# Six banks instead of eight for the first joint layer of an attention and MLP kernel, halves of a two-bank tile kept apart in the second, and a new order table

## The chip, the cores and the metric

The kernel runs on one core of a Trainium2 chip. What is measured is the device time of one execution in microseconds (us). The kernel before took 593.06 us (median of three runs, 593.02 to 594.8).

## The reference

Attention over 4 batches of 12 heads with 448 positions and head width 64, with a tanh cap on the scores, then two dense layers over the 1792 tokens (768 to 2048 to 768) with a smooth gate between them. All inputs and outputs are float32.

```python
scores = scale * np.matmul(q, k.transpose(0, 1, 3, 2))
scores = cap * np.tanh(scores / cap)
scores = scores - np.max(scores, axis=-1, keepdims=True)
attn = np.exp(scores)
attn = attn / (np.sum(attn, axis=-1, keepdims=True) + 1e-09)
attn_out = np.matmul(attn, v)
...
x = attn_out.transpose(0, 2, 1, 3).reshape(B * S, H * D)
h = x @ w_in
g = np.where(h >= 1, h, np.where(h <= -1, 0.0, (h + 1) ** 2 / 4))
out = g @ w_out
```

## The kernel before

Every product of the dense layers is made of three matmuls with fp16 operands, since each operand is held as a high and a low half (high times high, low times high, high times low; `product`, L761 to 773). Work goes by pairs of heads, 24 in all: scores on PE, tanh and exponential on ACT, sums on DVE, the product with v on PE, then `norm` and `divide` (copies on ACT, L486, a chain on DVE, L498, and a spread on PE, L509).

Batches 0 and 1 go through the two dense layers plainly (L579 to 617). Batches 2 and 3 are done together with fewer products: sums and differences of their tiles and of blocks of the weights are made first (on DVE; split into halves on ACT and DVE, L522, L525, L795, L796), and each product then serves two blocks. In the **first joint layer** (L836 to 868) turn i of eight takes three accumulators y, x and z from `new_bank`. Product after product is added into y; between them ACT copies y out (`copy_out`, L778), and PE adds the next product to y only when that copy has read it. `plus` (DVE, L783) adds an accumulator to such a copy. `gate` (ACT L589 and L590, DVE L591) makes the input of the second layer. In the **second joint layer** (L893 to 946) three accumulators `ys`, three `xbs`, three `wbs` and three `zbs` take their names from a list `banks`; `scaled` (ACT, L894) copies out, `plus` adds and DMAs store the results. The last product is cut, for its last two chunks, into columns 0 to 255 and 256 to 447 of the same bank, each part with its own `plus` and its own DMA.

PE's accumulators lie in eight banks of PSUM. Four are tiles of their own (f0, f1, av0, t0); the other four are halves of two tiles, s0 and s1 (here s0a, s0b, s1a, s1b). In the program's names (as f0_140, s0_138) the halves of s0 read alike. Before the change `new_bank` goes round all eight, in the order f0, f1, s0a, s0b, s1a, s1b, av0, t0, three a turn: turn 6 has y in s0a, x in s0b, z in s1a, turn 7 has y in s1b, x in av0, z in t0. The second layer goes on in the same round: ys are f0, f1, s0a; xbs s0b, s1a, s1b; wbs av0, t0, s0b; zbs s1a, s1b, av0.

The order of the instructions on each engine is not made by loops. Each step is put into a plan with a cost; the order in which steps are issued, and the engine of those that may run on ACT or DVE, stands in a packed table, ORDER, that was written out beforehand. `Plan.order` unpacks it. The costs in the code went into making that table; when the program is built they do nothing.

At the end `verdict` (L315 to 329) makes one number, fi, from range checks. Each engine loads it (L1409) and branches over a general version of the program (L1410), which doesn't run here.

Of the kernel before, what the change touches and what calls it, by code (L numbers as in the profile page):

```python
# [21 lines left out]
P = 128  # L22
# [68 lines left out]
    "#m8_DpTQL<j<?|t%!MWJSNH`Vzzg^dpTJA_6JNpaSPUQHAMh*w3H#tRM8v095#PXmcn_8EK0d<A_!geSWBdT`pgums5!ePJ(Hne#PvI~48ya9ke2#CiDptct_!{5iJB*C~;1i63QSm!e!M4~AKVVu+"
    "ho3Pr0lvU#h)CE7qhVu=kL^+6D@=gtaS3+7FZeG;$Eef<|Hfq08($*hNBj#DVj}E=eX$>Az)$!cJ7PxcgfS>Fj>MAKAEQxj%!8#cI%UF9m;?vlXq=9jaRwg1u{Z|vVm>U5NpU8Y!LJyTfZ|YooE;Vj"
    "(KuX+WpNoU$2qtOXJG*>h}E$Mmcz}s5^Lf)Y>Kt8HpZpFv;wzadEAP1FdnVKX4o8C;5Y1yEpa<`!5vr^2jVvDLxZptCZ~hg6}#bJRMZ`Z;CP&XhcE#}p@fu@4r32wYK^hzD8{Cra42dzf<NOiOhl<@"
    "BBr4X)D!3892$o6P-qgK#|s#rCSzLaOBXRU4aa_T3A4}?oQnNvJ}y8*DQF=Mpdn;wHLk&(xCjT5qs2Is*5WQ)hwJe;W~9ZGiPF(9+JL)p5beRecml)GM!bx}sW_FOeYhX9(g+$!N$CofqVP1A5>sZH"
    "M@eWtoy4n{gVIw3%0;zl2}PvRw2=1D0y<2m@H8%^Y*dyiQb`&`qiGrCrZF^@uHhoOjyWk0jid2Yi6+nrT1k0nB2A*nG==if89a-tXf>^&TR4@b(O$ZNRcSfh#Qe06_EP~`OWA2U-J&B@j*e0pT1S=X"
    "7_Fxbw2@BGZ*+j_&`Byth3OzwqfNA#X3!RzNp)!}m8WfVoMzF#RF4i(1*%WCsUcOTrgVx<(-}HTHK-8PqC3=ps?c5fof^?STBn-PY-&#TsWCmEBGiJm(=W7xcG9o3UbUoi^b`F|=jj4nq)T*}uF!XC"
    "MUUtseWK6wkZMv}dQ4wvvuZ+LsWt7QEoz6_r$C{4LQm-#eIrs=DUM>*p0tXqo>M#(U%j9sssp{GS9Fc8(;w7^ZcswikvdUl`jcMM8|p$k)mswvlQPPxpVd3suin!J<y1IzNrhJt)CbzCl+sv~cBw>a"
    "lRB>wtBvX}il{ED3#uy}P)XEoilh>#q$-(8p(3j&DyrJ1wyTROrMjZ7tG_9limuM6Z>k#=qwds$VyMrm9LH2u_@FwfQmJ;-la8t6Dz!?ZcB@{LR;5$NReF^{-B34akBX%-s=ey2`mTD@Np(}*Q@^N8"
    ">X16DGOK^+syd;5Raw-1^+4rO#HZAAl~p}dk5pn_%-Pf-eOf(M*OcO0%JNyod`=Zsw^eNQn|h)0s#hwX%C7!U`PCf-oP;$yj>NyK$o!{D&N29jdaa(S94e>ErE)9eXDS6(=Qk=G3&-Rr{9c9U0?Keo"
    "E}~wlX#7F_rJ{3Gj>WOLs4A@rs<d286;~0sj4Gi@s&xET6;cs7GnZB6RC)EUs=;yjovNwg@kjMZ#o;WRfRl1oPR12fMU|6lb1p8WQgM2&rBd_X>K|2G)#3PDN2TFPs;;Wbl~oVU##K~9uE~u!H#b);"  # L100
    "R6_ou5^+zir!sIJ&dY_krOM73xjENYnYgN|rdp{MT!f2q1Jzn}RXMmAx8#PZIG5n+sx8;!l3YWzQTceSD#&eBY0l4$R4wkyjkz5c;4<7;eO2956IGwPauaT+`f+>JfXj1t)s*}5ARfVmxvA>It9cDK"
    ";~uJ+>Zv-Yj%qCrRu#FI>ZB@gD{jqgxIOn#ow&2=%zafCHGs$QKpx3mxEJ^4!Q4*`QN2}J?ym-@?mU!7sY*Or9o9qD5q(+@<8?etjpFe<gopD$HC%Pz(L902sN;H~8pDTpB3I>(JeDW(BsGOcsExdy"
# [71 lines left out]
def fast_body(ctx, tc, flag, qkp, vp, cap, w_in, w_out, out):  # L174
# [61 lines left out]
    def act(n, fn, r, w):  # L236
        either(r, w, act_(n, fn))
# [1176 lines left out]
```

## Time and profile before

| | |
|---|---|
| Median of three runs | 593.06 us (593.02 to 594.8) |
| Profiled execution | 595.54 us, of which 593.4 us is the span of its instructions |
| PE busy | 573.6 us (97%) |
| DVE busy | 517.6 us (87%) |
| ACT busy | 419.7 us (71%) |
| Mean granted clock of TensorE | 0.995 |

PE is busy for nearly the whole span, so the views that matter are those that say where it isn't: its waits, and the stretches by window. Busy time of a matmul group includes its pipelined end, so that the next row on PE may start before the row above has run out. Times in the rows below are counted from the start of the span; the profiled execution's own time is 2.14 us longer than its span.

### The profile page before, as it was taken

Reading aid. Unit: us, or ns where it says so; the run is one execution under the profiler, and the core shown is the slowest. Engines: PE = TensorE matmul, PEld = TensorE weight load, DVE = VectorE, ACT = ScalarE, POOL = GpSimd, SP = SyncE. Lnnn points to the kernel's source line nnn. Section 1 sums busy time; section 2 is a strip of 40 time slices with the busy share of each in tenths; the row PEclk is TensorE's granted clock in tenths of the full one; section 3 lists DMA queues with packets and bytes.
Section 4 is the critical chain, followed back from the end, with each engine's and each line's share of the span. In section 5 each row is a group of like instructions: output and inputs, shape, how many; then the busy total and the mean of one; then the engine's idle time right before and its main releaser. Section 6 shows DMA issues by size and latency. Waiting matters only on the chain. (4 is left out here: it accounts for less than half of the span.)

```text
span 593.4 us, 10251 instructions
## 1 busy us (share of the span) xinstructions
PE 573.6 (97%) x3824; PEld 281.0 (47%) x3824; DVE 517.6 (87%) x1014; ACT 419.7 (71%) x705; POOL 1.3 (0%) x6
## 2 busy tenths in 40 slices
PE   7989999999999999999999999999999899999995
PEld 3334445454445544554444454445555444455543
DVE  7999999999999999999997865799999978999602
ACT  7999988787565689888989979366978766442000
POOL 0000000000000000000000000000000000000000
PEclk9999999999999999999999999999999999999998
DMA  8868748667877311133699999954755545743302
GB/s 303 321 227 291 273 160 298 214 235 266 276 255 255 112 65 60 65 99 105 201 326 289 334 329 304 291 195 139 225 202 199 176 143 160 236 136 121 114 0 85
DMA packets 56990, 119.92 MB, mean 202 GB/s; under 512 B 4962, under 2 KB 35426, under 8 KB 55394
## 3 DMA queue, kind: packets, MB, share of 16 engines
q1 hardware_dynamic: 56928, 119.16, 59.9%
q8 instruction: 32, 0.52, 0.4%
q14 instruction: 28, 0.23, 0.1%
q10 hardware_dynamic: 2, 0.00, 0.0%
HBM read 91.42 MB, written 27.72 MB: 201 GB/s over the span
## 5 line engine op out<-in xcount | busy, mean ns | idle before, releaser
L773 PEld LDWEIGHTS <-w 128*128 128x128 f16 x726 | 71.2, 98 | 74.3 <-issue 9.0
L395 ACT ACTIVATE e<-s,tsc 128x896 f32<-128x896 f32 (+1 forms) x96 | 85.4, 910 | 12.5 <-PE s L387 7.6
L396 ACT ACTIVATE e<-e,capb 128x896 f32<-128x896 f32 (+1 forms) x96 | 88.8, 948 | 0.5
L579 PE MATMUL f<-x,w 128*128 128x448 f16 x192 | 67.8, 353 | 0.1
L615 PE MATMUL f<-g,w 128*128 128x448 f16 x192 | 67.8, 353 | 0.0
L581 PE MATMUL f<-x,w 128*128 128x448 f16 x192 | 67.7, 352 | 0.0
L617 PE MATMUL f<-g,w 128*128 128x448 f16 x192 | 67.7, 352 | 0.0
L616 PE MATMUL f<-g,w 128*128 128x448 f16 x192 | 67.7, 352 | 0.0
L580 PE MATMUL f<-x,w 128*128 128x448 f16 x192 | 67.7, 352 | 0.0
L387 PE MATMUL s<-spl 64*128 64x448 f16 x432 | 49.6, 352 | 1.5 <-ACT e L395 1.5
L463 PE MATMUL av<-e,vt 128*64 128x448 f32 x216 | 45.8, 550 | 0.8 <-ACT xf L486 0.8
L590 ACT ACTIVATE r<-r 128x448 f32<-128x448 f32 x64 | 36.1, 573 | 1.1
L387 PEld LDWEIGHTS <-spl 64*128 64x128 f16 x432 | 17.4, 94 | 29.6 <-issue 17.6
L276 ACT ACTIVATE w<-z 128x768 f16<-128x768 f32 (+1 forms) x22 | 20.7, 943 | 13.6 <-DVE z L273 13.6
L589 ACT ACTIVATE r<-f,half 128x448 f32<-128x448 f32 x34 | 21.4, 630 | 12.2 <-PE f L581 11.0
L277 DVE SCALAR_TENSOR_TENSOR w<-z,w 128x768 f16<-128x768 f32 (+1 forms) x28 | 29.7, 1062 | 0.3
L579 PEld LDWEIGHTS <-w 128*128 128x128 f16 x192 | 18.8, 98 | 19.4 <-issue 3.9
L615 PEld LDWEIGHTS <-w 128*128 128x128 f16 x192 | 18.8, 98 | 18.7 <-issue 3.0
L617 PEld LDWEIGHTS <-w 128*128 128x128 f16 x192 | 18.8, 98 | 17.5
L581 PEld LDWEIGHTS <-w 128*128 128x128 f16 x192 | 18.8, 98 | 17.6
L424 DVE TENSOR_TENSOR sums<-e,e 128x896 f32<-128x896 f32 x24 | 26.0, 1084 | 0.7 <-ACT e L396 0.7
L346 DVE SCALAR_TENSOR_TENSOR spl<-qkr,spl 128x896 f16<-128x896 f32 (+2 forms) x25 | 26.1, 1047 | 0.3
(318 smaller groups left out, 1141.5 us busy)
## 6 DMA issues: line engine op xcount, KB each, us to landing
w<-w_in SPq DMA_DIRECT2D x32, 384.0 KB, 5.6
z<-w_out SPq DMA_DIRECT2D x24, 512.0 KB, 5.6
w<-w_in SPq DMA_DIRECT2D x14, 768.0 KB, 7.0
qkr<-qkp SPq DMA_DIRECT2D x23, 448.0 KB, 4.7
vt<-vp SPq DMA_DIRECT2D x24, 320.0 KB, 4.5
w<-w_out SPq DMA_DIRECT2D x7, 1024.0 KB, 5.9
zd<-z SPq DMA_DIRECT2D x16, 384.0 KB, 2.6
zd<-z SPq DMA_DIRECT2D x12, 512.0 KB, 4.1
```

What stands on the lines that cost most here:

```text
L387: T.matmul(s[:, j, :S], lhsT=t[h, a, S + c * P:S + (c + 1) * P], rhs=t[h, b, :S], start=(i == 0), stop=(i == 2))
L395: act(w * S + 60, lambda: A.activation(e[:, :w] if c < 3 else e[:, 0].rearrange("p (h s) -> p h s", h=2), s[:, :w, :S] if c < 3 else s[:, ...
L396: act(w * S + 125, lambda: A.activation(e[:, :w], e[:, :w], AF.Exp, scale=capb), ek + [("tsc", None)], ek)
L463: T.matmul(a[h, :S], lhsT=vt[:, j * 3 + c], rhs=e[:, j], start=(c == 0), stop=(c == 2), skip_group_check=True)
L579: T.matmul(ph, lhsT=w1[:, 0, fc, c], rhs=x[c][0][:, 0], start=(c == 0), stop=False)
L580: T.matmul(ph, lhsT=w1[:, 1, fc, c], rhs=x[c][0][:, 0], start=False, stop=False)
L581: T.matmul(ph, lhsT=w1[:, 0, fc, c], rhs=x[c][0][:, 1], start=False, stop=(c == NCC - 1))
L590: act(S, lambda: A.activation(r, r, AF.Square, scale=math.sqrt(WS * XS / GS)), rk, rk)
L615: T.matmul(po, lhsT=hi[:, fc], rhs=gv[:, 0], start=(fc == 0), stop=False)
L616: T.matmul(po, lhsT=lo[:, fc], rhs=gv[:, 0], start=False, stop=False)
L617: T.matmul(po, lhsT=hi[:, fc], rhs=gv[:, 1], start=False, stop=(fc == NFC - 1))
L773: T.matmul(t, lhsT=lhs(x, c), rhs=rhs[c][0][:, y], start=(first and c == i == 0), stop=(stop and c == n - 1 and i == 2), skip_group_check= ...
```

## The change

The table ORDER is a new one. The first joint layer takes its accumulators from six banks of six different tiles (f0, f1, s0a, av0, t0, s1a): even turns have f0, f1, s0a for y, x, z, odd turns av0, t0, s1a. In the second layer ys are f0, f1, av0; xbs s0a, s0b, s1a; wbs t0, s1b, s0a; zbs s0b, s1a, t0. The last product stops in its bank, t0, before the last two chunks and has a `plus` of all 448 columns; the last two chunks go into f0 (columns 0 to 255) and f1 (256 to 447) and are added from there. A dozen costs of the plan are other numbers; two of them are shown. Lines stand one lower after L703.

```diff
...
-    "c-l=^1E3_yvW<w0jLaO{wr$(CZQHhO+qUi9v9TC)ceoh;TU9;#e&0rQB5=-$$hsX11Q23FH~@$P3Jk=Bcn}{fB!CEz5VpBQkQkCcQV0*pAUQ;a6p#`KO29u55mJGJ)Q|?!LON&&f{`FSl!S_q0ir`j"
...
+    "c-mEW1ArvS^L0dIWMt;rwr$(CZQHhO+cs{^yEP7Ln|EvTzV51?`~AP3>8Ywj;KhrVH2|?7HVDK4191UCK|BZt@gV{b2qu7p5D^kVVn_lEksv8pNCr_LIi!G;5FR3fgH#X=QbQU@3nic=q=T|h3MxW+"
...
-        act(width + 110, lambda: A.activation(hi.bitcast(F32), hi.bitcast(F32), AF.Relu, accum_out=chp[:, i, part:part + 1]), zk, zk + [("chp", (i, part))])
+        act(width + 155, lambda: A.activation(hi.bitcast(F32), hi.bitcast(F32), AF.Relu, accum_out=chp[:, i, part:part + 1]), zk, zk + [("chp", (i, part))])
...
-        pe(20 + 800 * len(cs), run, [k for c in cs for k in st["e", n, c][1]] + vk + (ak if cs[0] else []), ak, "aa")
+        pe(-10 + 772 * len(cs), run, [k for c in cs for k in st["e", n, c][1]] + vk + (ak if cs[0] else []), ak, "aa")
...
     retire([("s1", None)], pbk[4:6])
     turn["pb"] = -1
+    pb1, pb1k = [[l[i] for i in (0, 1, 2, 6, 7, 4)] for l in (pbs, pbk)]
 
     def take_from(name, tiles, keys):
         turn[name] = i = (turn.get(name, -1) + 1) % len(tiles)
         return tiles[i], [(keys[i], None)]
 
     def new_bank():
-        t, k = take_from("pb", pbs, pbk)
+        t, k = take_from("pb", pb1, pb1k)
         return t[:, :S], k
...
-        act(S, (lambda: A.copy(u, t)) if scale == 1.0 else lambda: A.activation(u, t, AF.Copy, scale=scale), k, ukey)
+        act(S - 67, (lambda: A.copy(u, t)) if scale == 1.0 else lambda: A.activation(u, t, AF.Copy, scale=scale), k, ukey)
...
-    banks = [new_bank() for _ in range(8)]
+    banks = [(pbs[i][:, :S], [(pbk[i], None)]) for i in (0, 1, 6, 2, 3, 4, 7, 5)]
     ys, xbs, wbs, zbs = banks[:3], banks[3:6], [banks[6], banks[7], banks[3]], [banks[4], banks[5], banks[6]]
...
     def steps(bank, first, lhs, rhs, r):
-        for c0 in range(0, HF, STEP):
-            product(bank, first and c0 == 0, c0 + STEP == HF, lambda x, c, c0=c0: lhs(x, c0 + c), rhs[c0:c0 + STEP], r)
+        for c0 in range(0, len(rhs), STEP):
+            product(bank, first and c0 == 0, c0 + STEP == len(rhs), lambda x, c, c0=c0: lhs(x, c0 + c), rhs[c0:c0 + STEP], r)
...
         steps(zbs[i], True, wv(i, 0), gb(2), wqk(i, 0))
         plus(zbs[i], u4s[i], out_scale)
         store(3, HE + i, u4s[i])
-        if i < HE - 1:
-            steps(zbs[i], False, wv(HE + i, 1), gb(3), wqk(HE + i, 1))
-            plus(zbs[i], u2s[i], out_scale)
+        last = i == HE - 1
+        steps(zbs[i], False, wv(HE + i, 1), gb(3)[:HF - STEP * last], wqk(HE + i, 1))
+        plus(zbs[i], u2s[i], out_scale)
+        if not last:
             store(2, HE + i, u2s[i])
-    (t, k), (u, ukey), lhs, rhs = zbs[i], u2s[i], wv(HE + i, 1), gb(3)
-    for c0 in range(0, HF - STEP, STEP):
-        product(zbs[i], False, False, lambda x, c, c0=c0: lhs(x, c0 + c), rhs[c0:c0 + STEP], wqk(HE + i, 1))
-    for q, cols in enumerate(LAST):
-        bank_, part = (t[:, cols], [(k[0][0], q)]), (u[:, cols], [(ukey[0][0], q)])
-        product(bank_, False, True, lambda x, c: lhs(x, HF - STEP + c), [(g[:, :, cols], key) for g, key in rhs[HF - STEP:]], wqk(HE + i, 1))
-        plus(bank_, part, out_scale)
-        dma(4 * P * (cols.stop - cols.start), lambda cols=cols: M.dma_start(out[DM - P:, 2 * S + cols.start:2 * S + cols.stop], u[:, cols]), part[1], [("out", (2, HE + i, q))])
+            continue
+        u, ukey = u2s[i]
+        for q, cols in enumerate(LAST):
+            bank_, part = (ys[q][0][:, cols], ys[q][1]), (u[:, cols], [(ukey[0][0], q)])
+            product(bank_, True, True, lambda x, c, f=wv(HE + i, 1): f(x, HF - STEP + c), [(g[:, :, cols], key) for g, key in gb(3)[HF - STEP:]], wqk(HE + i, 1))
+            plus(bank_, part, out_scale)
+            dma(4 * P * (cols.stop - cols.start), lambda cols=cols, u=u: M.dma_start(out[DM - P:, 2 * S + cols.start:2 * S + cols.stop], u[:, cols]), part[1], [("out", (2, HE + i, q))])
     retire([(k, None) for k in xlk[6:]], ["z1"])
     verdict()
     with tc.manual_schedule():
```

On PE at the end of the first joint layer, before. The first column is the line; s0, s1, f0, f1, av0 and t0 are accumulators, w2_0 and w2_1 weights of the second layer, qkr, spl and w1 weights of the first, and what follows the arrow is the pair of operands (one row of several chunks shown, each of three matmuls).

```order
L773 MATMUL s0_138<-e1_96,qkr0_89 128x448
...
L773 MATMUL s1_139<-g15_127,qkr1_90 128x448
...
L773 MATMUL s0_138<-x3_108,qkr1_90 128x448
...
L773 MATMUL s0_138<-g1_113,w2_0_80 128x448
...
L773 MATMUL f1_141<-g16_128,w2_1_81 128x448
...
L773 MATMUL s0_138<-x0_105,qkr0_89 128x448
...
L773 MATMUL s1_139<-e0_95,w1_79 128x448
```

The same place after the change:

```order
L774 MATMUL f0_140<-x3_108,qkr1_90 128x448
...
L774 MATMUL f1_141<-g16_128,w2_1_81 128x448
...
L774 MATMUL f1_141<-g8_120,w2_1_81 128x448
...
L774 MATMUL av0_142<-x5_110,w1_79 128x448
...
L774 MATMUL f0_140<-x0_105,qkr0_89 128x448
...
L774 MATMUL s0_138<-e0_95,w1_79 128x448
...
L774 MATMUL s0_138<-g7_119,w2_1_81 128x448
```

Turn 6's y lay in s0a, and the next product on PE went into s0b; now it lies in f0, and twelve matmuls into f1 and nine into av0 stand between y's third product (the row with x3) and its fourth (the row with x0).

On PE in the second layer, before. ys[2] is the s0 of the rows with w2_5 and of those with w1_79 as their second operand; wbs[2] is the s0 of the rows with w2_2.

```order
L773 MATMUL s0_138<-sums0_103,w1_79 128x448
...
L773 MATMUL s0_138<-g0_112,w2_2_82 128x448
...
L773 MATMUL s0_138<-w1_79,w2_5_85 128x448
...
L773 MATMUL s0_138<-sums0_103,w2_5_85 128x448
...
L773 MATMUL s0_138<-w1_79,w2_2_82 128x448
...
L773 MATMUL s1_139<-x3_108,w2_4_84 128x448
```

The same place after the change:

```order
L774 MATMUL av0_142<-sums0_103,w1_79 128x448
...
L774 MATMUL s1_139<-raw_86,w2_4_84 128x448
...
L774 MATMUL t0_143<-x5_110,w2_2_82 128x448
...
L774 MATMUL av0_142<-w1_79,w2_5_85 128x448
...
L774 MATMUL s0_138<-g0_112,w2_2_82 128x448
...
L774 MATMUL t0_143<-e2_97,w2_2_82 128x448
```

ys[2] moved from s0a to av0, and products into other tiles stand between its parts.

On DVE at the end of the program, before:

```order
L326 SCALAR_TENSOR_TENSOR rr0_129<-z1_88,rr0_129 1x4
L328 TENSOR_REDUCE rr0_129<-rr0_129 1x1
L783 SCALAR_TENSOR_TENSOR wr1_137<-av0_142,wr1_137 128x256
L329 TENSOR_SCALAR fi_59<-rr0_129,f_58 1x1
L783 SCALAR_TENSOR_TENSOR wr1_137<-av0_142,wr1_137 128x192
L1409 TENSOR_LOAD fi_59
```

The same place after the change:

```order
L784 SCALAR_TENSOR_TENSOR wr1_137<-t0_143,wr1_137 128x448
L326 SCALAR_TENSOR_TENSOR rr0_129<-z1_88,rr0_129 1x2
L784 SCALAR_TENSOR_TENSOR wr1_137<-f0_140,wr1_137 128x256
L784 SCALAR_TENSOR_TENSOR wr1_137<-f1_141,wr1_137 128x192
L328 TENSOR_REDUCE rr0_129<-rr0_129 1x1
L329 TENSOR_SCALAR fi_59<-rr0_129,f_58 1x1
L1410 TENSOR_LOAD fi_59
```

The number fi, which stood ahead of the last `plus`, now stands behind it. On SP the load of fi stood between the last two DMAs, and now stands behind both.

## Rows read from the trace of the kernel before

**Rows 1.** Windows: stretch, its length, busy time per engine, clock, DMA share, GB/s

```profile
core 0: us, PE busy (x) PEld busy (x) DVE busy (x) ACT busy (x) POOL busy (x), PEclk, DMA share, GB/s
0.00:60.00 60.00, 53.46 (x509) 22.52 (x510) 54.69 (x143) 53.94 (x69) 0.66 (x5) 1.00 0.81 286
60.00:285.00 225.00, 225.00 (x1621) 110.63 (x1621) 221.19 (x337) 175.63 (x257) 0.00 (x0) 1.00 0.52 179
405.00:465.00 60.00, 60.00 (x319) 31.02 (x317) 57.74 (x118) 48.99 (x96) 0.00 (x0) 1.00 0.62 203
474.77:478.43 3.66, 3.66 (x12) 1.56 (x12) 3.53 (x9) 3.44 (x6) 0.00 (x0) 0.61 0.42 139
495.00:516.00 21.00, 19.26 (x100) 9.54 (x99) 18.45 (x41) 9.21 (x18) 0.00 (x0) 1.00 0.62 189
```

**Rows 2.** Waits of PE: line <- what ended it: total us, times, longest

```profile
PE s L773 <- ACT xf L778: 2.7, 1, 2.7
PE t L509 <- DVE mix L498: 2.2, 2, 1.9
...
PE s L773 <- ACT w L522: 1.2, 1, 1.2
...
PE s L773 <- ACT wr L894: 0.6, 1, 0.6
PE s L773 <- ACT xf L894: 0.6, 1, 0.6
...
PE s L773 <- ACT wr L778: 0.5, 1, 0.5
PE av L773 <- DVE w L796: 0.4, 1, 0.4
```

**Rows 3.** Timeline of PE at turn 6: start, duration, what [idle before]

```profile
470.77 1.30 PE L773 MATMUL s<-e,qkr 128*128 128x448 f16 x6
474.77 2.40 PE L773 MATMUL s<-g,w 128*128 128x448 f16 x6 [2.70 <-ACT xf L778]
476.96 1.64 PE L773 MATMUL f<-g,w 128*128 128x448 f16 x6
```

**Rows 4.** Timeline of ACT at the same place

```profile
474.20 0.51 ACT L778 COPY xf<-s 128x448 f32<-128x448 f32 x1
```

**Rows 5.** Timeline of PE and of DVE at turn 7's gate

```profile
489.27 1.86 PE L773 MATMUL s<-x,spl 128*128 128x448 f16 x9
...
497.42 0.62 DVE L591 SCALAR_TENSOR_TENSOR vt<-s,r 128x448 f32<-128x448 f32 x1 [2.23 <-PE s L773]
497.96 0.61 DVE L783 SCALAR_TENSOR_TENSOR wr<-t,wr 128x448 f32<-128x448 f32 x1
...
500.11 0.62 DVE L591 SCALAR_TENSOR_TENSOR wr<-wr,r 128x448 f32<-128x448 f32 x1
```

**Rows 6.** Timeline of PE, behind that gate

```profile
501.39 1.01 PE L773 MATMUL s<-w,w 128*128 128x448 f16 x3 [1.18 <-ACT w L522]
```

**Rows 7.** Timeline of all engines at the end

```profile
585.61 0.49 PE L773 MATMUL av<-sums,w 128*128 128x256 f16 x3
586.13 0.42 DVE L783 SCALAR_TENSOR_TENSOR wr<-av,wr 128x256 f32<-128x256 f32 x1 [2.73 <-PE av L773]
586.48 0.19 DVE L329 TENSOR_SCALAR fi<-rr,f 1x1 int32<-1x1 f32 x1
586.61 0.41 PE L773 MATMUL av<-e,w 128*128 128x192 f16 x3 [0.52 <-DVE wr L783]
...
587.30 0.36 DVE L783 SCALAR_TENSOR_TENSOR wr<-av,wr 128x192 f32<-128x192 f32 x1 [0.64 <-PE av L773]
```

**Rows 8.** The branch, by line: engine, operation, ns min/median/max, first and last start

```profile
L1410 PEldq COMPARE_BRANCH  x1: 3977/3977/3977, 587.3 to 587.3; - x1
...
L1410 DVEq EVENT_SEMAPHORE  x1: 21/21/21, 591.5 to 591.5; - x1
```

**Rows 9.** Timeline of PE in the head

```profile
31.52 0.35 PE L509 MATMUL t<-mix,sel 128*128 128x224 bf16 x2 [1.90 <-DVE mix L498]
31.80 0.97 PE L463 MATMUL av<-e,vt 128*64 128x448 f32 x4
```

More of the change, by code (lines that the diff above doesn't have):

```diff
@@ L91 @@
[L91 to L102, printed above, removed]
@@ new lines @@
+    "hz=Pb24sYokO>+>IVcU8p%PSsEYJwDg28N19%?~t_yjE=DpZE*PzJI?W3Z?p2ULKnPzN05ges5=YCsbRhb^HdgvX{(7urH@Xax~488(1skOziBeP{=H;WG?_e9#d(L3?Np_23J%f&B0lIzs`N1K*(_"
+    "w1zP-7KTG1_y#d>E{uSYP#BV9Hz)!>pa&F%agYT&z*LwBqhK0zf$>lbQs6w81jV5zbcgAX5*NdKSOC2sCiaHOFd8Pnen^cgpbt!eB@hey!b<1|OW^>_fHg1>20?%53Ikvv%!WfS3l_n0h>fdYEnI+K"
+    "VKp3vbx;Tg!!o!CX)rDhfsODRoP{HB5;j9BTn`5!9v*{p5C>;M1-t~OU<+)5({LV+!*#d}N1+X#fHSZawn0|h4m%(lZh)QeJ7mY*a0B+h73hUG;TPBi*YG+%fWmkc?!aC66MjNHyaf;89z24Zm;;Mo"
+    "QTz*@!Zmn-f53Kk3#Z|2xDPM!IqZcyco+YMocI|2ffrB=U%~^-g}3n)yoM+E5G&$7h=@<|9aO^CSR8NQGq{g$;61#BNB9ArVP$-SRj?|4gnRf3-(d-?j}0&qzQ<}98UKYS7!@1hCrpcgS1}qsM#M;z"
@@ new lines @@
+    "4hb7$bZm?5a0EVq`1lsn<7ZTu0iR=gOo0Dj6a0o5u_GqL{a6wcA!8|QgdZ?6eZdY`8aH8LEQ6h}H-5!FI1>9}Zp?$DFd0RqzcC3e!S9$C|HaYx5i{XwOo~4+ALhsYn4F@}Sd2z7XdEKNq|8_ViN;_-"
+    "9Ds4CI+n#6*c6*#Ka5L2(P=ssCq+y%P?OM7Oh75ACf35(G!tV{ZH!0dusj+{MYC`jmZ0X?0%zlLOhYX(9Ie2g*crRv9PC4NFd@~&%{UOZ;7SZngRm<mq6`$DTH#hqOWklVc1KIAFbVa*A$R~&Q%2f`"
+    "t#Ld~z=JpxGtnVDf{wOhPn?TMX)sO1c{mJHP&(Rylkg}W#xpn>v(Q-_j_0s1&BxWa02ksKJdY)53f88n*pGh4MYtAs;yU~T*JFRmOuyi-xC`gdZ@2-o(qbGyyKym<q9L>qkKs@nM#Jei?!kdHi1uP>"
+    "noD&kJ!PY^bOLkG2&zbb;z-(u^XMd&qcW73>e3P#MN26H&8JFKmCDm!SeY(hHCjdyDHr9Wi#VFb&{!Hr<7om-q)9ZHrqEQHM!RVNRiPDh3UkwRT22co57nbZl$R<{ecD6$s5&*IrnHg{(Is3(`Drz+"
@@ L131 @@
+    "x#Hi140$I5Ls;vE$zWhu*q2Z8RmJZI4`|OZ`^$V{V~EmTG5v~otU;f)!6?|*1kbmBL{eBN-uW9yS<vfW2?ps4HvC_mW`B2pMqU!&pJ-v^!vA%#cdoDxf~SU|^EB*q2|G{7mne@O-mS+_A3lcvbLs|#"
+    "E|{-h3D1|W1i@m5_~uJa(1rLC9CqUPO7E+>A3ys?MxZ}L{95^^aacrNH~3oTYXf_Y=@AM-C%D&s6oL~xrKbPXHF$V%=#7Sa`g?f$$fF;>-_G7b@Ido=-FpjwuyQhnBsbU)zEXI`{MV(xRfP@*Uv(+O"
+    "N$`$@kl|neKw;eWHH-eIHQ;ad&r1k<_wZHFCk8_(6aIfmkM<J"
 )
@@ L388, in qk @@
         parts = range(len(cuts(n)) if cs[-1] > 1 else 1)
-        pe(sum(570 if c < 3 else 385 for c in cs), run, [(k, (z, i)) for z in parts for i in range(2)], [x for c in cs for x in st["s", n, c][1]], "qr" if cs[-1] == 3 else "qq")
+        pe(sum(572 if c < 3 else 322 + 95 * (len(cs) > 1) for c in cs), run, [(k, (z, i)) for z in parts for i in range(2)], [x for c in cs for x in st["s", n, c][1]], "qr" if cs[-1] == 3 else "qq")
     def expo(n, c):
@@ L450, in run @@
                             T.matmul(a[h, :S], lhsT=vh[:, x, j * 3 + c], rhs=e[:, y, j], start=(c == x == y == 0), stop=(c == 2 and x == 1), skip_group_check=True)
-            pe(20 + 570 * len(cs), run, [k for c in cs for k in st["eh", n, c][1]] + vk + (ak if cs[0] else []), ak, "aa")
+            pe(32 + 570 * len(cs), run, [k for c in cs for k in st["eh", n, c][1]] + vk + (ak if cs[0] else []), ak, "aa")
             return
@@ L484, in run @@
                     T.matmul(t[q:q + 32, :S // 2], lhsT=w, rhs=m, start=(g == 0 and c is None), stop=(g == 1 and c == (late[-1] if late else None)), tile_position=(0, q))
-        pe(450 + 375 * len(late), run, mk + [k for c in late for k in st["e", n, c][1]] + [("ones", None), ("halves", None)] + (tk if g else []), tk, "tt")
-        act(S, lambda: A.copy(xf, a[:, :S]), ak, fk)
+        pe(402 + 385 * len(late), run, mk + [k for c in late for k in st["e", n, c][1]] + [("ones", None), ("halves", None)] + (tk if g else []), tk, "tt")
+        act(S - 67, lambda: A.copy(xf, a[:, :S]), ak, fk)
         if g:
```

75 lines of the change are left out of this document (38 added, 37 removed).

## The prediction

> **What bounds the kernel now.** I read the windows first [rows 1]. PE, DVE and ACT stand beside each other there: from 60 to 285 us PE is busy for all of 225.00, and from 405 to 465 for all of 60.00 with 319 matmuls, 0.188 us each at a granted clock of 1.00. PE is the bound, its matmuls are the same ones after the change, and a change of order can only give back time in which PE is idle or slow. So the next view is the list of PE's waits [rows 2], and then the timeline around each of the longer ones. The reader is to ask of each wait whether what it waits for is needed by the matmul that waits.
>
> Most of them are not. At 474.77 PE has waited 2.70 us for ACT's copy of turn 6's y [rows 3, 4], but the matmul goes into another bank, s0b, where nothing has to be copied; y lies in s0a, the other half of the same tile. The wait is for the tile. The twelve matmuls behind it run from 474.77 to 478.43 at a mean granted clock of 0.61, so for the most part at the lower level of 1.2 GHz [rows 1], after that idle time. The waits for L894 (twice 0.6) and for the copy wr L778 (0.5) have the same form: the waiting product goes into one half of s0, the copy reads the other [rows 2].
>
> The wait before 501.39 is the end of a longer chain. DVE's gate reading of turn 7's y, in s1b, has waited 2.23 us for a product into s1a [rows 5]. Behind it on DVE stands an addition of 0.61, behind that, by way of ACT, the next gate at 500.11, and behind that ACT's cast L522 that PE waits 1.18 us for [rows 6].
>
> **The change part by part.**
>
> *Clock and waits at turn 6.* y now lies in f0 and the product that follows in f1, tiles of their own. Between y's third and fourth product stand 12 and 9 matmuls, 21 x 0.188 = 3.95 us. PE's last matmul of the third product ended at 472.07 and the copy at 474.71, 2.64 us later [rows 3, 4]; 3.95 covers that, with 1.3 over. The wait of 2.7 goes. Twelve matmuls at 0.188 take 2.26 us and took 3.66; without an idle time before them I take the other clock, 1.4. The 1.4 rests on the clock falling after long waits only: waits of 1.90 and 1.18 [rows 9, 6] lie in stretches whose mean granted clock is 1.00 [rows 1]. If this cover fails, 2.7 and 1.4 stay. Sum: 4.1, bounds 0 and 4.1.
>
> *Waits for the other half of a tile.* With s0a and s1a alone in the first layer, the 0.5 goes; with ys[2] in av0, the 1.2 of L894 goes. ys[2] itself is read by ACT between two of its products; twelve matmuls (2.26 us) into s1 and t0 stand there now, where PE waited 0.6 with none, so nothing is late next. Sum: 1.7, bounds 0.5 and 1.7.
>
> *Turn 7's gate.* It no longer waits 2.23 for a neighbour, so the wait of 1.18 at the end of the chain goes. Next in line is the weight split L796 on DVE, for which PE waited 0.4 a little later [rows 2]; I leave that wait in. Sum: 1.2, bounds 0 and 1.6.
>
> *Six banks instead of eight.* A bank comes back after two turns, not after eight thirds of one. Counted in the new order, the matmuls between a bank's last product of one turn and its first two turns on are 36 to 60 (6.8 to 11.3 us), but once, for av0 from turn 5 to turn 7, only 21, 3.95 us. There PE waits for a gate on DVE. Before, turn 7's last product ended at 491.13 and its gate at 498.04, 6.9 later, of which 2.23 was the wait for the neighbour [rows 5]: 4.7 without it. PE then waits 4.7 - 3.95 = 0.8. Behind the waiting matmul stand all products of turn 7 on PE. In a shorter form the same can happen where only six to nine matmuls stand between a product and the next into the same accumulator; for these I take another 0.4, the size of the wait for L796. Cost 1.2, bounds 0 and 13.4 (the last rival below).
>
> The Trainium skill, in Perfetto Trace Analysis, section Matmul Optimizations, asks for all 8 PSUM banks to be used so that as much as possible runs side by side; the change leaves two idle in the first joint layer. By the rule eight in rotation would be the better choice, and the trace agrees only in part: the copies of [rows 3, 4] kept a seventh and an eighth bank from being used while they ran. By the rule alone nothing of the 8.0 below would arrive; I don't follow it here, and it is a rival.
>
> *The last product.* Its second half of columns waited 0.5 for DVE to read the first half of the same bank [rows 7]; in f0 and f1 that wait goes. A `plus` of 448 columns is added, 0.61 as at 497.96 [rows 5], in a stretch where DVE had idled 2.73 [rows 7]. But fi is now made after the last `plus`, before it was done at 586.67. PE's branch takes 3.98 us from 587.30 and ends at 591.28, and DVE goes on at 591.5 [rows 8]. The end of PE's 256 columns lies at 586.10. In the new order the 192 columns follow at once (586.76, as 0.66 passed from 586.61 to 587.27), the `plus` lasts 0.36 to 587.15, and a reduction (0.1, an estimate: half of L329's time) and L329 (0.19) bring fi to 587.4, 0.7 later than before. The branch of PE would end at 592.0, 0.5 behind DVE's 591.5. I take a loss of 0.4, between that and 0 (if the branch is not what ends last); bounds a gain of 0.5 (PE's wait, if the last DMA ends it all) and a loss of 0.7 (all of fi's delay).
>
> *The head.* PE waited 1.90 at 31.52 for DVE's chain of `divide` [rows 9]. In the new order a product of the same kind as that of 31.80 (0.97) stands ahead of the first L509. It fills 1.0 of the wait. ACT is busy for 53.94 of the first 60 us and DVE for 54.69 [rows 1], so more than that can hardly come; bounds 0 and 1.9.
>
> *Costs in the code, fewer or more casts on DVE against ACT.* The costs do nothing on the chip. A cast moved between the two is hidden behind PE, as PE is idle nowhere from 60 to 285 us; if that cover were gone it would cost about 0.6, as DVE's work of 448 columns does [rows 5].
>
> *Sum.* 4.1 + 1.7 + 1.2 + 1.0 = 8.0 given back, 1.2 + 0.4 lost, 6.4 net. From the profiled execution, 595.54 with a span of 593.4 and 2.14 around it, that is 589.1. The median of the runs lies 2.48 below the profiled execution, at 593.06; from there it is 586.7.
>
> **The rivals.**
>
> *DVE takes over the bound (589.8).* From 405 to 465 us DVE is busy for 57.74 of 60, from 495 to 516 for 18.45 of 21 [rows 1]. When PE no longer stands still at turn 6, DVE has to keep up through turns 6 and 7 with no time to recover. All that it surely gains itself is the 2.23 of the false wait. Then of the 5.3 of turn 6 and 7's gate (4.1 + 1.2) only 2.2 arrives: 6.4 - 3.1 = 3.3. For it: these shares, and the wait for L796 that stays. Against it: DVE had waited for PE (2.23) and not only PE for DVE.
>
> *Other things are late at the same places (593.0).* The matmul at 474.77 may also wait for operands that come just as late, as ACT was busy with other work until 474.20; the wait then carries another name. What remains is the 0.5 and the 1.2, less 1.6: no change. Against it: ACT's work ahead of the copy is not what PE's next matmul reads by its row.
>
> *Six banks are too few (slower, 598.9).* If gates lag by 9.5 us behind their last product (the measured 6.9 and the 2.6 of a copy queued in front), PE waits 9.5 less the cover wherever this is short: 5.5 at the cover of 3.95, 2.7 at 6.8, 1.0 twice at 8.5, 0.4 at 9.1: 10.6, and twice 1.4 of clock behind the two long ones, 13.4 in all. In place of the 1.2 that is 593.06 - 8.0 + 0.4 + 13.4 = 598.9. It decides from a lag of about 8.4. Against it: 2.23 of the 6.9 is the wait that goes, so that the lag should be nearer to 4.7. The rule of the Trainium skill on the banks, named above, points to this side.
>
> **How the numbers follow.** Forecast 0.66; DVE bound 0.20; no change 0.08; slower 0.06. Two runs of this kernel within 0.3% (1.8 us) can't be told apart. The first two cases are faster by more than that, at 586.7 and 589.8; so 0.86, 0.08, 0.06. The range reaches down to 583.0, where nothing of the 1.6 is lost and the head gives all its 1.9 and more is found in the order, and up to 591.5, past DVE as the bound; the last two cases lie outside.
>
> **What would show it.** Right: no wait of PE over 1 us from 390 to 585; a clock of 1.00 from 465 to 480; no waits of PE for L894's line; the matmul into f1 directly behind that into f0 at the end; the gate's reading of turn 7 within 5 us of its last product. Wrong: PE waits for DVE's gate line in front of products into av0 or f0 (six banks too few); DVE without idle time from 465 to 516 and PE waiting for L796 or its casts (DVE bound); a new wait where 2.70 stood.

## The result and the profile after

The kernel after took 585.86 us (median of four runs, 584.97 to 586.69) against 593.93 (593.02 to 597.16) for the kernel before in the same comparison; the ratio is 0.9854, with a 95% interval of [0.9812, 0.9896]. Measured again in the last series of experiments it was 585.04 against 594.67, ratio 0.9842 [0.9826, 0.9859]. So the change gives 8.1 to 9.6 us by the medians, and 9.4 with a margin of 1 by the narrower interval. 586.7 was forecast, a change of 6.4 from 593.06. The time that an execution takes beyond its span is 2.1 to 2.3 us in all 56 runs of the kernel before that stood beside the experiments, and 2.2 to 3.3 in the nine of the kernel after; so the span fell a little more than the time, from 592.5 to 582.3 in the last series.

First the list of PE's waits, the whole of it (the columns are those of [rows 2]):

```profile
PE s L387 <- ACT e L395: 1.6, 3, 1.0
PE f L639 <- POOL x L633: 1.2, 1, 1.2
PE t L509 <- DVE mix L498: 0.7, 1, 0.7
PE av L463 <- ACT e L396: 0.2, 1, 0.2
PE t L484 <- DVE sums L424: 0.2, 1, 0.2
PE s L384 <- ACT e L395: 0.2, 1, 0.2
```

All of these lie in the first 60 us. No line of the joint layers is left: the 2.7, the 1.2, the 0.5 and both 0.6 of [rows 2] are gone, and so is the 0.4 for L796 that I had left in. Against [rows 1] the windows show the same:

```profile
0.00:60.00 60.00, 55.50 (x514) 22.95 (x515) 54.74 (x142) 54.32 (x70) 0.66 (x5) 1.00 0.81 292
...
390.00:465.00 75.00, 75.00 (x398) 38.83 (x397) 72.00 (x150) 57.77 (x112) 0.00 (x0) 1.00 0.60 192
465.00:516.00 51.00, 51.00 (x272) 26.35 (x270) 50.26 (x108) 34.35 (x66) 0.00 (x0) 1.00 0.60 192
516.00:574.00 58.00, 58.00 (x308) 30.01 (x307) 33.56 (x83) 8.03 (x15) 0.69 (x1) 1.00 0.29 98
```

PE is busy for all of 390 to 574 us, at a granted clock of 1.00 throughout. DVE is busy for 50.26 of the 51 us from 465 to 516: it comes close to PE, and doesn't hold it up.

Turn 6 and turn 7 on PE, then the gates of turn 5 and of turn 7 on DVE:

```profile
466.79 1.30 PE L774 MATMUL f<-e,qkr 128*128 128x448 f16 x6
467.92 2.43 PE L774 MATMUL f<-g,w 128*128 128x448 f16 x12
470.19 0.73 PE L774 MATMUL av<-x,w 128*128 128x448 f16 x3
...
483.81 1.87 PE L774 MATMUL av<-x,spl 128*128 128x448 f16 x9
```

```profile
468.17 0.61 DVE L591 SCALAR_TENSOR_TENSOR wr<-av,r 128x448 f32<-128x448 f32 x1
...
488.03 0.61 DVE L591 SCALAR_TENSOR_TENSOR vt<-av,r 128x448 f32<-128x448 f32 x1
```

Twelve matmuls stand behind y's third product, as in [rows 3]; there they took 3.66 us at a clock of 0.61 [rows 1], here they pass from 467.92 to 470.19, in 2.27. Turn 5's gate has read av0 by 468.78, 1.4 before PE comes back to that bank at 470.19. Turn 7's gate ends at 488.64, 3.0 behind the end of its last product (485.68), where it was 6.9 in [rows 5].

The end of the program:

```profile
574.61 0.49 PE L774 MATMUL f<-e,w 128*128 128x256 f16 x3
...
575.27 0.41 PE L774 MATMUL f<-e,w 128*128 128x192 f16 x3
...
575.54 0.78 DVE L784 SCALAR_TENSOR_TENSOR wr<-f,wr 128x256 f32<-128x256 f32 x2
575.99 0.81 SPq L947 DMA_DIRECT2D out<-wr  x2
...
576.45 0.20 DVE L329 TENSOR_SCALAR fi<-rr,f 1x1 int32<-1x1 f32 x1
```

The wait of [rows 7] in front of the 192 columns is gone, and the last addition ends at 576.3. But from the first product of 256 columns (574.61) to the end of the span (583.4) 8.8 us pass; in the kernel before these were 8.1 (from 585.28 to 593.4). This part became longer, though SP, the engine that ends last, branches at almost the same distance from that product as before: 3.1 us behind it, 3.0 in the kernel before. What grew is the time from SP's branch to its next step, 3.8 against 3.1 (rows in the experiments with the early verdict). From that step to the end 1.9 us pass in every trace of this case.

### The profile page after: what moved, and what is told of

It reads as the page before. It is cut to its first block, busy times and chain, and to the rows that moved or that the text cites. A ratio compares the mean times of both kernels' runs of the same rounds, so it can differ in the third digit from the quotient of the medians.

```text
span 583.4 us, 10253 instructions
## 1 busy us (share of the span) xinstructions
PE 571.3 (98%) x3824; PEld 281.0 (48%) x3824; DVE 518.6 (89%) x1017; ACT 420.9 (72%) x703; POOL 1.3 (0%) x6
## 4 chain that ended last, share of the span: by engine, by line
PE 53%; DVE 4%; ACT 1%; issue 0%; ACTq 0%
PE s L774 12%; PE f L774 11%; PE av L774 7%; PE t L774 3%; PE f L615 3%; PE f L616 3%; PE f L617 3%; PE av L463 2%; PE s L387 2%; PE f L579 1%; PE f L580 1%; PE f L581 1%; PE av L369 1%; PE t L484 1%; DVE wr L591 1%; DVE g L525 0%
## 5 line engine op out<-in xcount | busy, mean ns | idle before, releaser
L774 PEld LDWEIGHTS <-w 128*128 128x128 f16 x726 | 71.0, 98 | 65.4
L589 ACT ACTIVATE r<-f,half 128x448 f32<-128x448 f32 x36 | 22.6, 627 | 9.1 <-PE f L581 8.5
L579 PEld LDWEIGHTS <-w 128*128 128x128 f16 x192 | 18.8, 98 | 19.4 <-issue 3.6
L615 PEld LDWEIGHTS <-w 128*128 128x128 f16 x192 | 18.8, 98 | 18.2 <-issue 2.3
L617 PEld LDWEIGHTS <-w 128*128 128x128 f16 x192 | 18.8, 98 | 17.5
L581 PEld LDWEIGHTS <-w 128*128 128x128 f16 x192 | 18.8, 98 | 17.5
L580 PEld LDWEIGHTS <-w 128*128 128x128 f16 x192 | 18.8, 98 | 16.1 <-issue 0.4
```

Of the source, the lines that this page charges most:

```text
L579: T.matmul(ph, lhsT=w1[:, 0, fc, c], rhs=x[c][0][:, 0], start=(c == 0), stop=False)
L580: T.matmul(ph, lhsT=w1[:, 1, fc, c], rhs=x[c][0][:, 0], start=False, stop=False)
L581: T.matmul(ph, lhsT=w1[:, 0, fc, c], rhs=x[c][0][:, 1], start=False, stop=(c == NCC - 1))
L615: T.matmul(po, lhsT=hi[:, fc], rhs=gv[:, 0], start=(fc == 0), stop=False)
L617: T.matmul(po, lhsT=hi[:, fc], rhs=gv[:, 1], start=False, stop=(fc == NFC - 1))
L774: T.matmul(t, lhsT=lhs(x, c), rhs=rhs[c][0][:, y], start=(first and c == i == 0), stop=(stop and c == n - 1 and i == 2), skip_group_check= ...
```

## The experiments

The theory at the start was that of the prediction: PE waited for the other half of a tile. Rivals: DVE sets the pace of the joint layers anyway; or only the new order matters.

**Two banks exchanged in the kernel before.** The order is untouched.

```diff
+    pbs, pbk = [[l[i] for i in (0, 1, 2, 6, 4, 5, 3, 7)] for l in (pbs, pbk)]
     turn["pb"] = -1
```

> The kernel before, its order untouched, with two of its eight accumulator banks exchanged (s0b and av0), so that turn 6's y (s0a) and the product behind it no longer lie in one tile; turn 7's y and the product behind it (s1b, s1a) still do. Theory one, that PE waited for the tile and not for the bank: the waits of 2.7, 0.5 and twice 0.6 go and the clock stays at its upper level, 5.8 us faster (4.5 to 6.5), with the wait of 1.2 near 501 still there. Rival one, that DVE bounds these turns: 2 to 3.5 faster, and PE waits for DVE's weight splits or gates. Rival two, that only the new order table frees these places: within 1 of before, with a wait of about 2.7 at the same place.

Measured: 592.03, ratio 0.9952 [0.9934, 0.9970], 2.9 us faster. PE's timeline at turn 6, then its longest waits in the joint layers:

```profile
471.75 1.30 PE L774 MATMUL s<-e,qkr 128*128 128x448 f16 x6
472.88 1.30 PE L774 MATMUL av<-g,w 128*128 128x448 f16 x6
...
475.75 0.92 PE L774 MATMUL s<-x,qkr 128*128 128x448 f16 x4 [0.43 <-ACT xf L779]
```

```profile
PE s L774 <- ACT r L590: 1.6, 1, 1.6
...
PE s L774 <- DVE qkr L797: 0.6, 1, 0.6
```

With another tile the product follows y's at once (472.88), so the 2.7 was for the tile. But half of the gain doesn't arrive: PE waits 0.43 for the same copy where it really needs it, 0.6 for a weight split on DVE, and 1.6 more. The view puts the 1.6 down to ACT, whose work ended last, at 481.99. In the program the waiting product doesn't depend on that work; it depends on DVE's addition, which ended at 481.98:

```profile
481.36 0.62 DVE L784 SCALAR_TENSOR_TENSOR vt<-s,vt 128x448 f32<-128x448 f32 x1
```

```profile
482.04 0.73 PE L774 MATMUL s<-x,spl 128*128 128x448 f16 x3 [1.59 <-ACT r L590]
```

The addition reads turn 6's z, in s1a, and the product is one of turn 7's y, in s1b: the halves of s1 still meet. A wait of 0.62 at 421.35 is of the same form, with a product into s0a and a copy that reads s0b. So 2.2 of the 2.9 us that are missing are again waits for the other half of a tile, and the longer of them is as long as it is because DVE makes two weight splits ahead of its addition. The first theory is right about the wait; what it had wrong is that this exchange leaves no other such wait behind.

**All halves four places apart, in the kernel before.**

```diff
+    pbs, pbk = [[l[i] for i in (0, 1, 2, 4, 6, 7, 3, 5)] for l in (pbs, pbk)]
     turn["pb"] = -1
```

> The kernel before, its order untouched, with the eight banks permuted so that the halves of a tile are four places apart in the rotation; turn 7's gate no longer shares a tile with the product behind it either. Theory one: as in the run with two banks exchanged, and the 1.2 near 501 goes too: 7.0 us faster (5.5 to 7.5). DVE as the bound: 2 to 3.5 faster. The order table alone: within 1 of before.

Measured: 595.73, ratio 1.0007 [0.9994, 1.0020]. Theory one expected 7.0 faster and fails. The old waits are replaced by others:

```profile
465.73 0.62 DVE L784 SCALAR_TENSOR_TENSOR vt<-s,vt 128x448 f32<-128x448 f32 x1
```

```profile
466.40 2.14 PE L774 MATMUL s<-x,spl 128*128 128x448 f16 x8 [2.41 <-DVE vt L784]
...
503.51 1.01 PE L774 MATMUL s<-w,w 128*128 128x448 f16 x3 [2.04 <-ACT w L522]
```

The time that theory one gave fails here, its mechanism doesn't: the wait of 2.41 is again for the other half, as the addition reads s1a and the product goes into s1b. The 2.04 is for an operand, at the place where [rows 6] has 1.18. The mean granted clock from 465 to 516 us is 0.93. With the order fixed, moving the pairs moved the waits.

**The kernel after with av0 and s0b exchanged.**

```diff
-    pb1, pb1k = [[l[i] for i in (0, 1, 2, 6, 7, 4)] for l in (pbs, pbk)]
+    pb1, pb1k = [[l[i] for i in (0, 1, 2, 3, 7, 4)] for l in (pbs, pbk)]
...
-    banks = [(pbs[i][:, :S], [(pbk[i], None)]) for i in (0, 1, 6, 2, 3, 4, 7, 5)]
+    banks = [(pbs[i][:, :S], [(pbk[i], None)]) for i in (0, 1, 3, 2, 6, 4, 7, 5)]
```

> The kernel after, its order untouched, with av0 and s0b exchanged, so that y of the odd turns (s0b) and z of the even turns (s0a) lie in one tile again; six banks as before this edit. In the order some seven products go into one half directly behind a product into the other. Theory one: a wait of 0.6 to 2.6 us at each, 5 to 12 us slower than the kernel after. Rival, that the gain is the order table's and the sharing of a tile costs nothing: within 1 of the kernel after.

Measured: 605.11, ratio to the kernel before 1.0170 [1.0144, 1.0196]; that is 19 us slower than the kernel after (605.11 less 585.86), more than expected. ACT and PE at the longest wait:

```profile
417.44 0.63 ACT L589 ACTIVATE r<-s,half 128x448 f32<-128x448 f32 x1 [4.57 <-PE s L774]
...
420.69 0.51 ACT L779 COPY xf<-f 128x448 f32<-128x448 f32 x1
...
421.25 0.53 PE L774 MATMUL f<-x,qkr 128*128 128x448 f16 x1 [3.85 <-ACT xf L779]
```

ACT's gate reading of s0b waits 4.57 us for PE's product into s0a, the other half of the same tile; the copy of f0 stands behind it on ACT; PE then waits 3.85 for that copy, in a bank that shares nothing with either. This is one reason why the price was too low: a shared tile also stops the reading engine, and what is queued behind it. The clock is another: the listed waits of PE in the joint layers come to 12.9 us, and the mean granted clock is 0.93 from 405 to 465 us and 0.98 from 465 to 516, where it is 1.00 in the kernel after.

**The banks of after in the order of before.** Steps that would stand ahead of one they need are moved behind it, which concerns 10 of the steps; all others keep their place.

```diff
+    pb1, pb1k = [[l[i] for i in (0, 1, 2, 6, 7, 4)] for l in (pbs, pbk)]
...
-        t, k = take_from("pb", pbs, pbk)
+        t, k = take_from("pb", pb1, pb1k)
...
-    banks = [new_bank() for _ in range(8)]
+    banks = [(pbs[i][:, :S], [(pbk[i], None)]) for i in (0, 1, 6, 2, 3, 4, 7, 5)]
```

> The order of before with the banks of after (six of six tiles in the first joint layer, the new ones in the second); steps that would stand ahead of a step they need are moved behind it, all others keep their place; the end of the last product is as before. No two halves of a tile are in turn here. Theory two, that the banks and the order only work together: the gates of the old order come too late for six banks, 3 to 12 us slower than before. Rival, that the banks alone do it: 4 to 6 faster than before.

Measured: 605.90, ratio 1.0168 [1.0149, 1.0188], 10 us slower than before. PE waits for DVE's additions and gates:

```profile
PE s L793 <- DVE vt L803: 3.0, 1, 3.0
...
PE f L793 <- DVE vt L803: 2.5, 1, 2.5
...
PE av L793 <- DVE xf L610: 1.9, 1, 1.9
```

These three come to 7.4 us, and in each the addition or gate reads the bank that the product waits for. So the third rival of the prediction, six banks too few, is what happens in the old order: 10 us slower than before, where the rival had 5.8 (598.9 against 593.06). Banks and order are one change: the new banks in the old order cost 10 us, a shared tile in the new order 19, both together give 9. The new order with the eight banks of before was not run, so what the order alone would do is not shown.

**The wait at turn 6 filled with matmuls that nobody needs.**

```diff
         def run():
+            for _ in range(fill):
+                T.matmul(fs[1][:, :S], lhsT=lhs(0, 0), rhs=rhs[0][0][:, 0], start=True, stop=True)
...
-        steps(xbs[i], True, wv(i, 1), ga(2, 1), wqk(i, 1))
+        steps(xbs[i], True, wv(i, 1), ga(2, 1), wqk(i, 1), 14 * (i == 0))
```

> The kernel before with 14 matmuls of 448 columns put in front of the product that waits 2.7 us at 474.77; they go into f1, whose content nobody needs any more. They fill the wait and do nothing else. If the lower clock behind it comes of PE's idle time: granted clock 1.00 through this stretch and 1.4 us faster (0.8 to 2.0), with the following twelve matmuls in 2.3 us. Rival, that the clock falls there for another reason: the clock falls as before, and the time is within 0.5 of before or up to 1 longer.

Measured: 593.64, ratio 0.9984 [0.9969, 0.9998], 1.0 us faster (0.1 to 1.8).

```profile
470.69 2.81 PE L772 MATMUL f<-g,w 128*128 128x448 f16 x14
473.56 1.29 PE L775 MATMUL s<-g,w 128*128 128x448 f16 x6
474.69 1.30 PE L775 MATMUL f<-g,w 128*128 128x448 f16 x6
475.82 1.87 PE L775 MATMUL s<-x,qkr 128*128 128x448 f16 x9
```

```profile
465.00:480.00 15.00, 14.87 (x79) 7.41 (x78) 14.50 (x30) 9.70 (x18) 0.00 (x0) 1.00 0.59 180
```

The twelve matmuls pass in 2.26 us at a clock of 1.00. This fits a clock that falls because of the idle time. So do the mean clocks of the runs: their median is 0.998 in these twelve and 0.995 in the 24 of the kernel before. But the interval of the time is wide, and the fall doesn't come in every execution: see the next run.

**The first 345 steps of the order from the other table**, once in the kernel before, once in the kernel after; the two tables are written here as lists.

```diff
-out = old                 # the kernel before
+out = new[:345] + [step for step in old if step not in new[:345]]
...
-out = new                 # the kernel after
+out = old[:345] + [step for step in new if step not in old[:345]]
```

> The kernel before with the first 345 steps of its order (about the first 60 us) taken from the new table, all else as before. If the head's gain is what the two traces show there (idle time of PE before 60 us 6.5 and then 4.5), 2.0 us faster than before (1.4 to 2.6). By the prediction's own term 1.0 (0.5 to 1.3). Rival: what is won in the head is lost again behind it, 0 (within 0.5).

Measured: 596.04, ratio 1.0018 [1.0001, 1.0034]: about 1 slower. In PE's timeline a new wait stands behind the place where the two orders meet:

```profile
81.22 0.59 PE L484 MATMUL t<-sums,ones 128*32 128x224 f32 x8 [1.25 <-DVE sums L427]
```

and at turn 6, where PE waits its 2.70 us as before, the window shows no fall of the clock:

```profile
465.00:480.00 15.00, 12.22 (x65) 6.05 (x64) 14.67 (x30) 10.78 (x20) 0.00 (x0) 1.00 0.52 160
```

> The kernel after with the first 345 steps of its order taken from the table of before, so that its joint layers alone are new. If head and joint layers are independent: 2.0 us slower than the kernel after, no wait of PE from 390 us to the end. Rival, that the new table hangs together: waits in the joint layers come back, 3 or more slower than after.

Measured: 586.66, ratio 0.9859 [0.9838, 0.9880], against 0.9854 and 0.9842 for the kernel after: 0.3 to 1.0 slower by the medians, within the margin; by the spans it is 1.4 (median 584.2, and 582.8 over the nine runs of the kernel after). No wait of PE came back from 390 us on, so the joint layers don't need the new head, and they bring nearly all of the gain. What the head itself is worth stays open: the intervals exclude neither 0 nor 2 us, and the first of these two runs paid 1.25 where its orders meet.

**The verdict ahead of the last additions, in the kernel after.** Rows of DVE and of SP:

```diff
+L326 SCALAR_TENSOR_TENSOR rr0_129<-z1_88,rr0_129 1x2
+L328 TENSOR_REDUCE rr0_129<-rr0_129 1x1
+L329 TENSOR_SCALAR fi_59<-rr0_129,f_58 1x1
 L784 SCALAR_TENSOR_TENSOR wr1_137<-t0_143,wr1_137 128x448
-L326 SCALAR_TENSOR_TENSOR rr0_129<-z1_88,rr0_129 1x2
 L784 SCALAR_TENSOR_TENSOR wr1_137<-f0_140,wr1_137 128x256
 L784 SCALAR_TENSOR_TENSOR wr1_137<-f1_141,wr1_137 128x192
-L328 TENSOR_REDUCE rr0_129<-rr0_129 1x1
-L329 TENSOR_SCALAR fi_59<-rr0_129,f_58 1x1
...
+L1410 TENSOR_LOAD fi_59
 L947 DMA out<-wr1_137 128x256
 L947 DMA out<-wr1_137 128x192
-L1410 TENSOR_LOAD fi_59
```

> The kernel after with the last three steps of the verdict (the last check, the reduction and fi) moved ahead of the last product's first addition, where DVE is idle for 2.8 us; on SP the load of fi then stands ahead of the last two DMAs. If the late fi is what costs at the end (in the kernel after 8.8 us pass from the first product of 256 columns to the end, in the kernel before 8.1): 0.7 us faster than after (0.4 to 1.3), the end again 8.1 or less behind that product. Rival, that the last DMAs or the engines' restart behind the branch decide: within 0.3 of after.

Measured: 583.34, ratio 0.9816 [0.9790, 0.9842]; more than the 0.7 expected. The end passes in 7.1 us (574.07 to 581.2) instead of 8.8. It was run a second time beside the unchanged kernel after:

> The kernel after, unchanged, to stand beside the other runs of this series: 585.9 (585 to 587.5).

Measured: 585.04, ratio 0.9842 [0.9826, 0.9859].

> The kernel after with the end of the verdict ahead of the last product's first addition, a second time and now beside the kernel after itself. If the first run's traces tell it (from the first product of 256 columns to the end 8.8 us in the kernel after, 7.1 there): 1.7 us faster than the run of the unchanged kernel (1.0 to 2.4). Rival, that the first run's gain was chance beyond the 0.7 forecast for it: 0.4 to 0.9 faster.

Measured: 583.26, ratio 0.9814 [0.9800, 0.9828], 1.8 faster than the kernel after in the same series, and the end passes in 6.8 us (573.58 to 580.35) where the unchanged kernel beside it takes 8.6 (573.68 to 582.30). The time beyond the span is back at 2.1 to 2.3 in all ten runs of this version. It beats both kernels. The branch by engine, first in the kernel after, then in the second run with the early verdict (columns as in [rows 8]; an engine's EVENT_SEMAPHORE is the first thing it does behind its branch):

```profile
L1411 SPq EVENT_SEMAPHORE  x8: 17/17/17, 581.5 to 582.1; - x8
...
L1411 DVEq COMPARE_BRANCH  x1: 72/72/72, 577.3 to 577.3; - x1
L1411 PEldq COMPARE_BRANCH  x1: 3633/3633/3633, 577.3 to 577.3; - x1
L1411 SPq COMPARE_BRANCH  x1: 50/50/50, 577.7 to 577.7; - x1
```

```profile
L1411 SPq EVENT_SEMAPHORE  x8: 17/17/17, 578.4 to 579.0; - x8
L1411 ACTq COMPARE_BRANCH  x1: 50/50/50, 572.3 to 572.3; - x1
...
L1411 PEldq COMPARE_BRANCH  x1: 3817/3817/3817, 573.1 to 573.1; - x1
...
L1411 SPq COMPARE_BRANCH  x1: 50/50/50, 575.9 to 575.9; - x1
```

In the kernel after all engines branch within 0.4 us, and SP goes on 3.8 later. With an early fi, PE's sequencer and ACT have branched while the last matmuls still run, and SP goes on 2.6 behind its branch, which itself lies 2.3 us behind the first product of 256 columns instead of 3.1. So of the 2.1 by which the end is shorter than in the kernel after, 0.8 is the earlier branch of SP and 1.2 the shorter time behind it.

**That version with the last product in one bank, as before.**

```diff
-        last = i == HE - 1
-        steps(zbs[i], False, wv(HE + i, 1), gb(3)[:HF - STEP * last], wqk(HE + i, 1))
...
+    (t, k), (u, ukey), lhs, rhs = zbs[i], u2s[i], wv(HE + i, 1), gb(3)
+    for c0 in range(0, HF - STEP, STEP):
+        product(zbs[i], False, False, lambda x, c, c0=c0: lhs(x, c0 + c), rhs[c0:c0 + STEP], wqk(HE + i, 1))
...
-            bank_, part = (ys[q][0][:, cols], ys[q][1]), (u[:, cols], [(ukey[0][0], q)])
+        bank_, part = (t[:, cols], [(k[0][0], q)]), (u[:, cols], [(ukey[0][0], q)])
```

> The run with the early verdict, with the last product as in the kernel before: its last two chunks in the bank of the others, t0, in two halves of columns, and no addition of 448 columns. If the two own banks are worth the wait they take away (0.52, and 0.16 for the pipeline to fill again): 0.5 to 0.9 us slower than with own banks, with a wait of 0.5 in front of the 192 columns. Rival, that the end of the program hides it: within 0.3.

Measured: 583.79, ratio 0.9821 [0.9806, 0.9835], 0.5 slower; the intervals overlap. PE doesn't wait, against what I expected, since both products stand ahead of the additions in the new order; so this run puts no price on the wait of 0.52. Instead DVE can begin only when PE is through with the bank:

```profile
575.49 0.69 DVE L784 SCALAR_TENSOR_TENSOR wr<-t,wr 128x256 f32<-128x256 f32 x2 [3.42 <-PE t L774]
```

**The early verdict in the kernel before.**

```diff
 L328 TENSOR_REDUCE rr0_129<-rr0_129 1x1
+L329 TENSOR_SCALAR fi_59<-rr0_129,f_58 1x1
 L783 SCALAR_TENSOR_TENSOR wr1_137<-av0_142,wr1_137 128x256
-L329 TENSOR_SCALAR fi_59<-rr0_129,f_58 1x1
 L783 SCALAR_TENSOR_TENSOR wr1_137<-av0_142,wr1_137 128x192
```

> The kernel before with the verdict's last check, reduction and fi ahead of the last product's additions. If the late fi holds up the restart of the engines there too: 0.3 to 1.0 us faster than before, with fi made near 583.6 instead of 586.5. Rival, that in the kernel before the last DMA decides: within 0.2.

Measured: 594.26, ratio 0.9998 [0.9984, 1.0012]. No gain is seen in the time, though the interval leaves room for 0.9, and the end is 0.6 shorter in the trace (584.25 to 591.69, 7.4 us). SP branches at 587.0 and goes on 2.7 us later:

```profile
L1410 SPq EVENT_SEMAPHORE  x8: 17/17/17, 589.8 to 590.3; - x8
```

The rival, that the last DMA decides in this kernel, is not excluded: that DMA was issued at 586.7 and landed 3.1 us later, at 589.8 as well. In the kernel after it is: the last DMA, issued at 576.4, landed 1.7 later, and SP went on at 581.5.

## Why the prediction was right, and where it was off

Between the two profiled executions the span fell by 10.0 us, from 593.4 to 583.4. PE's last matmul ends at 575.93 instead of 587.27, 11.3 earlier, and the rest became 1.4 longer. Of the 11.3, PE's idle time behind 60 us is 7.0 (7.1 before, 0.1 after) and the fall of the clock 1.4. Another 1.8 I had not counted. It lies in the joint layers' matmuls themselves, and 1.6 of it has a reason: a matmul of 448 columns shows 0.352 from start to end and the next one starts 0.188 after it, so that each wait costs 0.16 more than its number, and ten waits went from these layers. The other 1.1 is what small differences leave of the head's 2.0.

So the mechanism of the main terms was right, and the forecast change was too small: 6.4, where 8.1 and 9.6 were measured. The loss of 1.2 for the six banks didn't come, and the 1.8 had not been counted. That the time itself came within 0.8 us of the forecast is in part luck with the start: the kernel before was taken at 593.06, and in the comparisons its median was 593.93, 594.75, 595.02 and 594.67.

- *Turn 6 (4.1):* it arrived in full. The step's reason was half the story: the wait was for the tile, as the exchange of two banks shows, but in the old order half of the price came back, 2.2 us of it as waits for the other half of a tile at two other places. That the clock then stays up is likely and not settled: filling the wait gave 1.0 (0.1 to 1.8), and one profile shows the same wait with no fall.
- *The other halves (1.7) and turn 7's gate (1.2):* arrived, with the 0.4 on top that I had left in. Turn 7's gate lags 3.0 us, not 4.7.
- *Six banks (a loss of 1.2):* this step was mis-sized; it measured 0. At the shortest cover, 3.95 us, turn 5's gate was done after 2.4. I had taken the lag of the gate from the old order, and the new order has other work ahead of the gates; that this is the reason was not tested by itself. The sentence that two banks are idle in the first joint layer was wrong for one of them: products of the second layer go into s0b from 436.14 us. In the kernel before the first such product into s0b began at 474.77, and the first into any bank at 456.90.

```profile
436.14 1.30 PE L774 MATMUL s<-g,w 128*128 128x448 f16 x6
```

- *The rule of the Trainium skill on all 8 banks (Perfetto Trace Analysis, section Matmul Optimizations):* in this change it was no loss that the first layer uses six, as PE waits nowhere from 390 to 574 us. In the old order six cost 10 us, which is what the rule would say.
- *The head (1.0):* idle time of PE fell by 2.0 in the trace, while the kernel after with the old head is 0.3 to 1.0 slower by the medians and 1.4 by the spans. The term was of the right size, as far as this shows.
- *The last product and the end (a loss of 0.4):* 0.7 by the traces, from the first product of 256 columns on. The step named PE's branch as what would end last; it was not. PE's ended at 581.0, before SP went on at 581.5. Nor was the late fi what cost: SP's branch moved by less than 0.1 against the first product of 256 columns, and SP went on 3.8 behind it instead of 3.1. The size came near by luck; the wait named was the wrong one.
- *DVE as the bound (rival):* not in the kernel after, though DVE is at 50.26 of 51 us; in the old order with two banks exchanged the time fits it, with 2.9 instead of 5.8. DVE's late addition sets the longest new wait there, but the product waits for it only because it shares the tile.

## What to carry to other kernels

A wait between two banks of one tile is real to the program: look whether the bank that waits is the bank that is read, and count what stands in the queue of the reading engine too. The engine that a view names behind a wait is only the one that ended last; ask the program what the waiting instruction depends on. Banks and the order of issue are one decision: the new banks alone made the kernel slower, and the exchange of two banks alone left most of the gain behind. And a number that every engine loads before a branch should be ready before the last work, so that the engines which are done can branch while the others still work; this gave 1.8 us in the kernel after, and no gain was seen in the kernel before.

## What was not expected of the hardware

How long SP needs to go on behind its branch goes with how close the branches lie: 3.6 to 3.9 us in the four traces in which five engines branch within 0.4 (the kernel after and two of its variants), 3.1 to 3.3 in the six in which they are spread over 1.1 (the kernel before and five of its variants), and 2.6 to 2.7 in the four with an early fi. That the number of engines at once is the cause is not shown; PE's own branch takes 3.4 to 4.0 in all of them. And the same idle time of 2.70 us was followed by a lower clock in the profiled execution of before (0.61 over the next 3.66 us) and by none in that of the variant with the new head. Of the 39 runs of the kernel before in the first two series, the four with a mean clock of 0.998 took 592.6 to 593.1 us, the others 593.7 to 598.0.
